# A gated linear attention feeding a mixture of experts: transposed q and k of four chunks in half tiles, the gate's loads behind chunk 0's, and a new order of the first steps

## The chip, the core and the metric

The kernel runs on one core of a Trainium2 chip. The core has a tensor engine for matmuls (PE in the profile, PEld for its weight loads), a vector engine (DVE), a scalar engine (ACT), a GpSimd engine (POOL), and a sync engine whose queue (SP) issues all of this kernel's data transfers. Each engine works through its own list of instructions in order; semaphores make one wait for another. The metric is the device time of one execution in microseconds (us), the median of several runs.

## The reference

```python
def _attn_ref(q, k, v, alpha):            # q, k, v, alpha: [4, 8, 768, 48]
    state = np.zeros((B, H, D, D))
    for t in range(S):
        state = alpha[:, :, t, :, None] * state + np.einsum('bhd,bhe->bhde', k[:, :, t], v[:, :, t])
        y[:, :, t] = np.einsum('bhd,bhde->bhe', q[:, :, t], state)
    return y

def _moe_ref(x, w_gate, w1, w2):          # x: [3072, 384], 8 experts, hidden width 1024
    logits = x @ w_gate
    P = np.exp(logits - logits.max())
    for _ in range(8):
        P /= P.sum(1, keepdims=True) + 1e-09
        P /= P.sum(0, keepdims=True) + 1e-09
        P *= N / E
    for e in range(E):
        out += P[:, e:e + 1] * (np.maximum(x @ w1[e], 0.0) @ w2[e])
    return out
```

The attention's output, 3072 tokens of 8 heads by 48, is the `x` of the mixture of experts. All eight experts see all tokens, so the matmuls of the experts are most of the work.

## The kernel before

**Attention.** The 768 steps of a sequence are cut into chunks of 128 tokens, 24 chunks over the four sequences. Within a chunk the products of decays are built up by doubling: at level L (1, 2, 4, 8, 16, 32, 64) the scores between the two halves of each block of 2L tokens are made by matmuls, and then q's second halves and k's first halves are multiplied by the decays of the other half, in place. The first four chunks do this with q and k already transposed (`direct_chunk`, line 328); the others start from blocks of 16 tokens that DVE and POOL work out in the natural layout (`attn_block`, line 448, two chunks at once), go through DRAM and continue in `attn_chunk` (line 589). Both end in `attn_tail` (line 656), which adds the carried state, scales the result into two float16 tiles `xT` (a high and a low part) and works out the logits of the gate.

**A direct chunk, step by step.** A step is what runs up to the next `yield`. "c0.3" is the third step of chunk 0.

- Step 1 (lines 335 to 338): SP issues five loads, alpha into `AN`, k into `KN`, q into `QN`, and v in two parts.
- Step 2 (341 to 359): PE transposes alpha, k and q, four transposes each, one for each pair of heads (`psD`, `psTk`, `psQR`); ACT copies each result out of PSUM, and DVE multiplies q by alpha. q and k lie side by side in one tile `T2` ("T" in the profile), 4 pairs of heads by 128 tokens each.
- Step 3 (361 to 422): 64 matmuls of 32 by 32 scores into `psl`; DVE multiplies them by a mask into `A32` (shown as "A<-psl,same"). Then level 1.
- Steps 3 to 7, levels 1 to 16 (407 to 422): 64 small matmuls into other columns of `psl`; DVE takes the scores of the level before over into `A32` (`kept`, the profile's COPY_PREDICATED "A<-odd,psl"); `merge` (380) multiplies pairs of decays (`D`, on POOL in steps written with a capital letter, else on DVE) and then, in one DVE instruction of 128x512 elements, the halves of q and k ("T<-T,D").
- Steps 8 and 9, levels 32 and 64 (425 to 445): 16 and 8 matmuls, a merge each, and ACT copies into `A`.
- Steps 10 to 13: `attn_tail`. Step 12 writes `xT`, step 13 the logits, which need the gate's weights.

**Experts.** `load_expert` (line 165) brings in an expert of the first three: steps w0.1 and w0.2 issue the loads of w1 (16 transfers) and w2 (2 transfers) into rooms that later hold `xT`; two steps of squares on ACT, one that finds a scale, then four steps that split a quarter of w1 each into a high part (ACT) and a low part (DVE in steps written small, POOL after two ACT operations in steps with a capital letter). w0.9 ends w1, w0.16 ends w2. `moe_tile` (line 241) computes one expert for 128 or 256 tokens in pieces of PE work ("ps" in the profile); the results go to DRAM as `raw`. These pieces are the filler: a step "f" runs so many of them as 0.45 us of PE work stands for, if any are ready. A tile becomes ready when its expert's w1 is split and the `xT` of its tokens is written; its second half waits for w2.

**The order.** One list, `START` (line 40), says in which order the steps of the chunks (c), blocks (b), experts' weights (w), decays (d), gate (g) and filler (f) are written out, up to chunk 7; from there a repeated unit `UNIT` takes over. A step that comes too soon (`early_`, line 811) is put off. Each engine gets its instructions in this order. After the attention, the sinkhorn loop (line 877) and five more experts follow with matmuls alone (`first`, `second`), from about 815 us on.

**The gate.** `work_gate` (line 218) takes the four loads of the gate's weights, issued by SP at line 764 ahead of everything in `START`, through a maximum and a scale to two float16 tiles, in three steps g.1 to g.3.

Of the kernel before, what the change touches and what calls it, by code (L numbers as in the profile page):

```python
# [25 lines left out]
def tile_gla_moe(ctx: ExitStack, tc: tile.TileContext, q, k, v, alpha, wg, w1, w2, out):  # L26
# [301 lines left out]
    def direct_chunk(ch, got):  # L328
# [10 lines left out]
        yield  # L339

        def turned(x, tag, t=None):
# [38 lines left out]
        def merge(L, Dl, both=True):  # L380

            n = P // (2 * L)
            d = Dl.rearrange("p j (n z) -> p (j n) z", z=2)
# [1 line left out]
            (GE if lop[0] else VE).tensor_mul(Dn.rearrange("p j n -> p (j n)"), d[:, :, 0], d[:, :, 1])

            x = T2.rearrange("p a j (n z t) -> p a (j n) z t", z=2, t=L)
            if both:
                e = x[:, 0, 0, 1, 0]
                o = bass.AP(tensor=e.tensor, offset=e.offset,  # L390
                            ap=[e.ap[0], [NP * P - L, 2], [2 * L, NP * n], [1, L]])
                m = bass.AP(tensor=d.tensor, offset=d.offset, ap=[d.ap[0], [1, 2], [2, NP * n], [0, L]])
                VE.tensor_mul(o, o, m)
            else:
                o = x[:, 1, :, 0]
                VE.tensor_mul(o, o, d[:, :, 1:2].to_broadcast([P, NP * n, L]))
            return Dn
# [9 lines left out]
        for i in range(NLV):  # L407
# [3 lines left out]
            for j in range(NP):  # L411
                for g4 in range(4):
                    tok = slice(g4 * 32, (g4 + 1) * 32)
                    for r in range(2):
# [877 lines left out]
```

## Time and profile before

| | us |
|---|---|
| median of 3 runs | 1712.93 |
| lowest and highest run | 1710.33, 1715.35 |
| the profiled execution: its time | 1712.7 |
| its span, first to last instruction | 1711.0 |
| its ACT busy | 932.9 |
| its POOL busy | 340.4 |

The span is 1.7 us shorter than the time of that execution. In the rows of a timeline stand: start, duration, engine, line, operation, "output<-inputs", partitions by elements, the number of instructions merged into the row, and in brackets how long the engine had been idle and what ended it ("issue": nothing that the profile shows). Most lines are L58 or L67, those of two helpers that record every operation, so the tiles' names are what one goes by. A row that merges many matmuls gives the time from the first to the last.

### The profile page before, as it was taken

How to read it: one execution, taken by the hardware profiler on the slowest of the kernel's cores; microseconds unless marked ns; L12 is line 12 of the kernel's file. 1: busy time of each engine (PE TensorE's matmuls, PEld its weight loads, DVE VectorE, ACT ScalarE, POOL GpSimd, SP SyncE). 2: the span in 40 equal slices, each digit the busy share in tenths (PEclk: the TensorE clock that was granted, in tenths of full speed). 3: DMA queues.
4: the chain of work that ended last, by engine and by line, in shares of the span. 5: the costliest groups of instructions: out<-in, count | busy, mean ns of one | idle time of the engine just before them, and what ended most of it. 6: DMA issues, size and time to landing. Idle time of an engine off the chain costs nothing.

```text
span 1711.0 us, 54791 instructions
## 1 busy us (share of the span) xinstructions
PE 1619.5 (95%) x23585; PEld 1438.3 (84%) x23585; DVE 1277.9 (75%) x2983; ACT 932.9 (55%) x2246; POOL 340.4 (20%) x345
## 2 busy tenths in 40 slices
PE   5679999999999999999899999999999999999998
PEld 4566677777777777767799999999999999999998
DVE  4757777666666656356788989998899979887776
ACT  3457443333333333326677767766666666665554
POOL 3334255434443533038100000000000000000000
PEclk9889999999999999999999999999999999999999
DMA  7152441342244133021312142323332232111111
GB/s 179 39 135 88 100 94 39 90 101 68 57 105 99 46 78 74 20 61 61 87 56 94 49 121 85 122 85 104 99 124 69 66 84 94 57 57 57 57 57 48
DMA packets 175457, 137.19 MB, mean 80 GB/s; under 512 B 109808, under 2 KB 165360, under 8 KB 175216
## 3 DMA queue, kind: packets, MB, share of 16 engines
q1 hardware_dynamic: 175216, 133.71, 28.3%
q8 instruction: 184, 3.01, 0.7%
q14 instruction: 57, 0.47, 0.1%
HBM read 86.50 MB, written 47.17 MB: 78 GB/s over the span
## 4 chain that ended last, share of the span: by engine, by line
PE 71%; DVE 16%; ACT 4%; issue 4%; DMA 3%; POOL 2%; SPq 1%; ACTq 0%; DVEq 0%; POOLq 0%
PE ps L67 23%; PE p1a L67 11%; PE p2x L67 11%; PE p2y L67 6%; PE p1c L67 5%; PE p1d L67 4%; PE p2v L67 3%; DVE h L58 3%; PE psl L67 2%; PE psy L67 2%; DVE AB L58 2%; POOL tmp L58 2%; DMA w1f<-in_moe_w_dram 2%; DVE tmp L58 1%; ACT w L58 1%
## 5 line engine op out<-in xcount | busy, mean ns | idle before, releaser
L67 PEld LDWEIGHTS <-h 128*128 128x128 f16 x6768 | 579.6, 98 | 115.9 <-issue 10.8
L67 PEld LDWEIGHTS <-w 128*128 128x128 f16 x8424 | 598.9, 98 | 43.2 <-issue 9.4
L58 DVE TENSOR_TENSOR h<-hf,h 128x256 f16<-128x256 f32 x480 | 290.5, 616 | 31.2 <-ACT h L58 30.8
L67 PE MATMUL ps<-xT,w 128*128 128x256 f16 (+1 forms) x2664 | 303.9, 271 | 7.2 <-DVE h L58 3.8
L67 PE MATMUL ps<-w,h 128*128 128x384 f16 x1728 | 293.6, 327 | 4.1 <-DVE w L58 2.2
L67 PE MATMUL p2x<-w,h 128*128 128x192 f16 x2880 | 276.8, 246 | 3.6 <-DVE p2y L58 3.4
L58 ACT CAST h<-hf 128x256 f16<-128x256 f32 x480 | 252.1, 571 | 13.1 <-DVE hf L58 8.4
L58 DVE TENSOR_TENSOR hf<-hf 128x256 f32<-128x256 f32 x480 | 182.1, 421 | 50.1 <-ACT hf L58 45.7
L58 DVE SCALAR_TENSOR_TENSOR h<-ps,h 128x256 f16<-128x256 f32 (+1 forms) x296 | 116.1, 411 | 138.2 <-ACT h L58 137.6
L58 ACT ACTIVATE h<-ps 128x256 f16<-128x256 f32 (+1 forms) x296 | 109.1, 375 | 143.5 <-PE ps L67 142.7
L67 PE MATMUL p1a<-xT,w 128*128 128x128 f16 x2160 | 179.5, 219 | 0.0
L67 PEld LDWEIGHTS <-wx 128*128 128x128 f16 x2160 | 147.8, 98 | 17.6 <-issue 17.5
L67 PE MATMUL p1c<-xT,w 128*128 128x128 f16 x2160 | 160.5, 220 | 0.0
L58 POOL TENSOR_TENSOR tmp<-qt,kt 128x768 f32<-128x768 f32 (+1 forms) x80 | 125.2, 1568 | 160.8 <-DVE AB L58 86.8
L58 ACT ACTIVATE hf<-p1d 128x256 f32<-128x256 f32 x120 | 45.8, 382 | 178.9 <-DVE h L58 148.8
L58 ACT COPY r<-ps 128x384 f32<-128x384 f32 x72 | 34.3, 478 | 194.1 <-PE ps L67 151.8
L67 PE MATMUL p2y<-w,h 128*128 128x192 f16 x1440 | 138.5, 246 | 1.2 <-ACT p2y L58 1.2
L67 PE MATMUL p1a<-xc,wx 128*128 128x128 f16 x1440 | 120.3, 220 | 15.3 <-ACT v L58 14.9
L58 DVE TENSOR_REDUCE AB<-tmp 128x16 f32<-128x768 f32 (+2 forms) x90 | 80.7, 904 | 49.0 <-POOL tmp L58 48.7
L67 PE MATMUL p1d<-xT,w 128*128 128x128 f16 x720 | 79.7, 220 | 0.0
L67 PE MATMUL p1d<-xT,wx 128*128 128x128 f16 x720 | 79.5, 220 | 0.0
L67 PE MATMUL p1a<-xc,w 128*128 128x128 f16 x720 | 79.4, 219 | 0.0
(208 smaller groups left out, 1969.4 us busy)
## 6 DMA issues: line engine op xcount, KB each, us to landing
accd<-acc SPq DMA_DIRECT2D x48, 384.0 KB, 2.5
acc<-accd SPq DMA_DIRECT2D x48, 384.0 KB, 3.3
raw<-r SPq DMA_DIRECT2D x72, 192.0 KB, 1.9
ri<-raw SPq DMA_DIRECT2D x72, 192.0 KB, 3.3
w1f<-in_moe_w_dram SPq DMA_DIRECT2D x20, 384.0 KB, 7.0
w2f<-in_moe_w_dram SPq DMA_DIRECT2D x5, 1536.0 KB, 7.2
VN<-in_v_dram SPq DMA_DIRECT2D x48, 96.0 KB, 3.1
xT<-in_moe_w_dram SPq DMA_DIRECT2D x6, 768.0 KB, 5.3
```

What stands on the lines that cost most here:

```text
L58: r = f(*a, **k_)
L67: tc.keep_in_program_order(nc.tensor.matmul(out_, lhsT, rhs, start=start, stop=stop, **k_))
```

## The change

Three edits go together.

First, `T2` becomes a list of two tiles, `T0` and `T1`, each with q and k of two pairs of heads. The copy of k out of PSUM and the product of q with alpha are made in two halves; every level writes the 32 matmuls of one half, that half's multiplication, then the 32 matmuls of the other half, `kept` and the second multiplication; the product of the decays comes last. The arithmetic and the number of matmuls stay.

```diff
-        T2 = fp.tile([P, 2, NP, P], F32, tag="T", name=f"T_{nm}")
-        QT, KT = T2[:, 0], T2[:, 1]
-        turned(kn[:, c], "Tk", KT)
+        HJ = NP // 2
+        T2 = [fp.tile([P, 2, HJ, P], F32, tag=f"T{z}", name=f"T{z}_{nm}") for z in range(2)]
+        psk, _ = turned(kn[:, c], "Tk", T2, 1)
         psq, QR = turned(qn[:, c], "QR")
-        VE.tensor_mul(QT.rearrange("p j t -> p (j t)"), psq, Dl.rearrange("p j t -> p (j t)"))
+        for z in range(2):
+            VE.tensor_mul(T2[z][:, 0], half(psq, z), Dl[:, z * HJ:(z + 1) * HJ])
...
         for i in range(NLV):
             L = 1 << i
...
-            for j in range(NP):
-                for g4 in range(4):
-                    tok = slice(g4 * 32, (g4 + 1) * 32)
-                    for r in range(2):
...
-            if i:
-                kept(i - 1)
-            Dl = merge(L, Dl)
+            Dn, part, deeper = merge(L, Dl)
+            for z in range(2):
+                Qz = odds(z, L)
+                for jj in range(HJ):
+                    for g4 in range(4):
+                        tok = slice(g4 * 32, (g4 + 1) * 32)
+                        for r in range(2):
+                            pr = slice(r * DP, r * DP + D)
+                            o = (z * HJ + jj) * P + 32 + i * 16
+                            mm(psl[r][tok, o:o + 16].rearrange("p (n t) -> p n t", t=L), T2[z][pr, 1, jj, tok],
+                               Qz[pr, jj, g4 * w:(g4 + 1) * w])
+                if z and i:
+                    kept(i - 1)
+                part(z)
+            deeper()
+            Dl = Dn
             yield
```

`part(z)` is the multiplication of `merge` for one of the two tiles, and `deeper` the product of the decays; levels 32 and 64 are rewritten in the same way.

Second, the gate's four loads become the first step of `work_gate`, which now has four steps; step 13 of a direct chunk waits for the fourth.

```diff
     def work_gate(wgf):
+        for j in range(NP):
+            SP.dma_start(wgf[quarter(j)], rows_of(wg, j))
+        yield
...
     hold[0] = True
-    for j in range(NP):
-        SP.dma_start(wgf[quarter(j)], rows_of(wg, j))
...
-            return (n == 12 and m < ND and gates[0] < 3 or m >= ND and "dtot" not in got[m // NCH]
+            return (n == 12 and m < ND and gates[0] < 4 or m >= ND and "dtot" not in got[m // NCH]
```

Third, `START` is another list. Up to the step that writes chunk 3's `xT` the two lists run as follows; a capital letter is one of the list's, f(n) are n pieces of filler, and the f's that find nothing to run are left out. Before:

```
c0.1 C0.2 C0.3 C0.4 C1.1 c0.5 C1.2 C0.6 w0.1 c0.7 B2.1 C1.3 C2.1 W0.2 w0.3 c0.8 c1.4 w0.4 W0.5 C1.5 w0.6
c0.9 w0.7 C1.6 w0.8 C0.10 C2.2 C1.7 b2.2 C0.11 w0.9 W1.1 c1.8 c2.3 B2.3 C1.9 W0.10 C3.1 C1.10 B2.4 g.1
B2.5 b2.6 c2.4 c0.12 c1.11 f(2) b2.7 f(2) b2.8 f(4) c2.5 c1.12 w0.11 b2.9 C3.2 c2.6 C3.3 c2.7 c2.8 w0.12
C3.4 c2.9 W0.13 c3.5 c2.10 b2.10 w0.14 w0.15 c3.6 b2.11 g.2 W0.16 W1.2 W1.3 W1.4 f(8) W1.5 f(4) C3.7 f(4)
B2.12 C3.8 b2.13 B2.14 B2.15 c3.9 g.3 c0.13 c2.11 C2.12 C1.13 W1.6 W1.7 c3.10 c3.11 C3.12
```

After:

```
c0.1 c1.1 C0.2 c0.3 C0.4 c0.5 c1.2 g.1 w0.1 w0.2 c0.6 w0.3 c0.7 W0.4 c0.8 w0.5 c2.1 C1.3 C0.9 c1.4 C1.5
w0.6 b2.1 w0.7 w0.8 w0.9 w1.1 c1.6 c0.10 C2.2 B2.2 C1.7 C1.8 C0.11 B2.3 g.2 C1.9 b2.4 w0.10 c2.3 C1.10
b2.5 c3.1 c2.4 B2.6 c0.12 c1.11 f(2) b2.7 f(6) c2.5 B2.8 C2.6 C1.12 c3.2 W0.11 b2.9 C3.3 c2.7 W0.12 C2.8
c3.4 c3.5 W0.13 c2.9 B2.10 w0.14 w0.15 C2.10 b2.11 g.3 B2.12 c3.6 W0.16 W1.2 w1.3 W1.4 f(11) w1.5 C3.7 f(4)
C3.8 f(1) B2.13 B2.14 b2.15 C3.9 g.4 C0.13 C2.11 c2.12 c1.13 W1.6 C3.10 C3.11 C3.12
```

Behind that the list goes on to chunk 7 with small shifts of the same kind; the pieces of filler up to the step that writes chunk 7's `xT` are as many as before. `attn_tail` takes q and k as lists of pairs of heads, with no change of what it does.

More of the change, by code (lines that the diff above doesn't have):

```diff
@@ L339, in direct_chunk, with turned @@
         yield
-        def turned(x, tag, t=None):
+        half = lambda x, z: x.rearrange("p (z j t) -> p z j t", z=2, t=P)[:, z]
+        def turned(x, tag, t=None, a=0):
             ps = psa.tile([P, 512], F32, tag="psa", name=f"ps{tag}_{nm}")
@@ L384, in merge, with part @@
             Dn = fp.tile([P, NP, n], F32, tag=f"D{2 * L}", name=f"D{2 * L}_{nm}")
[L385 to L397, printed above, removed]
+            def part(z):
+                x = T2[z].rearrange("p a j (n z t) -> p a (j n) z t", z=2, t=L)
+                dz = d[:, z * HJ * n:(z + 1) * HJ * n]
+                if both:
+                    e = x[:, 0, 0, 1, 0]
+                    o = bass.AP(tensor=e.tensor, offset=e.offset,
+                                ap=[e.ap[0], [HJ * P - L, 2], [2 * L, HJ * n], [1, L]])
+                    m = bass.AP(tensor=dz.tensor, offset=dz.offset, ap=[dz.ap[0], [1, 2], [2, HJ * n], [0, L]])
+                    VE.tensor_mul(o, o, m)
+                else:
+                    o = x[:, 1, :, 0]
+                    VE.tensor_mul(o, o, dz[:, :, 1:2].to_broadcast([P, HJ * n, L]))
+            return Dn, part, lambda: (GE if lop[0] else VE).tensor_mul(Dn.rearrange("p j n -> p (j n)"),
+                                                                      d[:, :, 0], d[:, :, 1])
         def kept(i):
@@ L426, in direct_chunk @@
             room = [x.rearrange("p (j c) -> p j c", c=P)[:, :, at_:at_ + L] for x in psl]
-            Qz = QT.rearrange("p j (n z t) -> p j n z t", z=2, t=L)[:, :, :, 1]
-            Kz = KT.rearrange("p j (n z t) -> p j n z t", z=2, t=L)[:, :, :, 0]
-            for j in range(NP):
-                for n in range(P // (2 * L)):
-                    po = slice(n * 2 * L, n * 2 * L + L)
-                    for r in range(2):
-                        pr = slice(r * DP, r * DP + D)
-                        mm(room[r][po, j], Kz[pr, j, n], Qz[pr, j, n])
-            Dl = merge(L, Dl, L < 64 or ch > 0)
+            Dn, part, deeper = merge(L, Dl, L < 64 or ch > 0)
+            for z in range(2):
+                Qz = odds(z, L)
+                Kz = T2[z][:, 1].rearrange("p j (n z t) -> p j n z t", z=2, t=L)[:, :, :, 0]
+                for jj in range(HJ):
+                    for n in range(P // (2 * L)):
+                        po = slice(n * 2 * L, n * 2 * L + L)
+                        for r in range(2):
+                            pr = slice(r * DP, r * DP + D)
+                            mm(room[r][po, z * HJ + jj], Kz[pr, jj, n], Qz[pr, jj, n])
+                part(z)
+            deeper()
+            Dl = Dn
             if L == 32:
@@ L445, in direct_chunk @@
             yield
-        yield from attn_tail(0, ch, vn[:, c], KT, QT, A, Dl[:, :, 0])
+        K_, Q_ = ([T2[j // HJ][:, a, j % HJ] for j in range(NP)] for a in (1, 0))
+        yield from attn_tail(0, ch, vn[:, c], K_, Q_, A, Dl[:, :, 0])
     def attn_block(b, u, got):
@@ L653, in attn_chunk @@
         yield
-        yield from attn_tail(b, ch, vn[:, c], KT, QT, A, got["dtot"][:, c])
+        K_, Q_ = ([x[:, j] for j in range(NP)] for x in (KT, QT))
+        yield from attn_tail(b, ch, vn[:, c], K_, Q_, A, got["dtot"][:, c])
     def attn_tail(b, ch, vn, KT, QT, A, dtot):
@@ L683, in attn_tail @@
             for j in range(NP):
-                tr(psk[:, j * P:(j + 1) * P], KT[:, j], ident)
+                tr(psk[:, j * P:(j + 1) * P], KT[j], ident)
             kb = ap2.tile([P, NP, P], F32, tag="kb", bufs=1, name=f"kb_{nm}")
@@ L763, in tile_gla_moe @@
     hold[0] = True
-    for j in range(NP):
-        SP.dma_start(wgf[quarter(j)], rows_of(wg, j))
     done = [99] * (ND // NCH) + [0] * (len(units) - ND // NCH)
```

19 lines of the change are left out of this document (10 added, 9 removed).

## The prediction

> **What bounds the kernel now.** I began with the page's first part, which says how much of the span each engine works.
>
> ```profile
> span 1711.0 us, 54791 instructions
> PE 1619.5 (95%) x23585; PEld 1438.3 (84%) x23585; DVE 1277.9 (75%) x2983; ACT 932.9 (55%) x2246; POOL 340.4 (20%) x345
> ```
>
> PE is idle for 1711.0 - 1619.5 = 91.5 us, and its work does not change here. Second came the table of busy time by stretch (start and end, length, then PE, PEld, DVE, ACT and POOL with their counts, PE's granted clock, DMA share, GB/s), cut where the stages change.
>
> ```profile
> 0.00:9.40 9.40, 2.88 (x12) 2.24 (x12) 2.49 (x12) 3.23 (x5) 7.65 (x35) 1.00 0.65 122
> 9.40:37.00 27.60, 14.95 (x766) 12.86 (x766) 13.59 (x36) 10.85 (x24) 2.33 (x5) 1.00 0.80 204
> 37.00:62.00 25.00, 17.99 (x463) 13.75 (x454) 13.80 (x31) 10.72 (x25) 7.89 (x9) 1.00 0.41 98
> 62.00:97.00 35.00, 21.78 (x731) 17.75 (x731) 27.62 (x68) 18.18 (x42) 15.29 (x14) 0.80 0.09 25
> 97.00:122.00 25.00, 18.79 (x332) 15.01 (x331) 13.84 (x45) 12.27 (x32) 8.47 (x8) 0.86 0.58 135
> 122.00:171.00 49.00, 45.02 (x506) 34.16 (x505) 33.94 (x73) 32.19 (x76) 19.74 (x16) 0.97 0.39 109
> 815.00:1711.00 896.00, 871.01 (x13007) 864.56 (x13005) 760.75 (x1891) 591.60 (x1361) 2.48 (x3) 1.00 0.26 80
> ```
>
> Half of the idle time, 122 - 76.4 = 45.6 us, lies ahead of 122 us; behind it PE is 92% busy and more. The reason is in the timeline of PE: the experts' first matmul comes at 61.67, but only two small tiles can be filled in until chunk 3's xT is written, and the large tiles begin behind it.
>
> ```profile
> 61.67 0.23 PE L67 MATMUL ps<-xT,w 128*128 128x128 f16 x1
> 122.66 9.58 PE L67 MATMUL ps<-xT,w 128*128 128x256 f16 x71 [0.55 <-DVE xT L58]
> ```
>
> So the first 122 us are bound by the way to chunk 3's xT (steps c0.1 to C3.12), not by PE's work. Every us taken from that way moves the rest forward, and the change touches little else. The waits of PE in that stretch (us in total, times, longest) show of what the way is made:
>
> ```profile
> PE psl L67 <- DVE A L58: 12.0, 7, 5.2
> PE psl L67 <- issue: 6.4, 4, 3.4
> PE psl L67 <- DVE T L58: 4.4, 5, 1.5
> ```
>
> PE's small matmuls wait 16.4 us for DVE (the merges T and the takeovers A), which is what the half tiles aim at, and 6.4 us for nothing that the profile shows.
>
> **Part 1, the gate's loads.** They are the first thing on SP, 1.81 us; behind the change they follow chunk 1's loads. Chunk 0's loads start 1.8 us earlier.
>
> ```profile
> 0.80 1.81 SPq L58 DMA_DIRECT2D wgf<-in_moe_w_gate_dram  x4
> 2.65 0.43 SPq L58 DMA_DIRECT2D AN<-in_alpha_dram  x1
> 4.88 0.56 POOL L58 MEMSET KN<- 128x256 f32 x2
> 5.87 1.09 PE L70 MATMUL psD<-ident,AN 128*128 128x128 f32 x4 [5.87 <-DMA AN<-in_alpha_dram]
> 6.75 1.06 PE L70 MATMUL psTk<-ident,KN 128*128 128x128 f32 x4
> ```
>
> Alpha's transposes wait for their load, but k's, at 6.75, also need POOL's zeroing of KN, which ends at 4.88 + 0.56 = 5.44 and stays. The gain is at most 6.75 - 5.44 = 1.3, and I take **-1.3**; its ends are -1.8 and 0. Nothing is lost behind: expert 0's loads on SP follow c0, c1 and the gate in either order, and the gate's weights are first used far later.
>
> **Part 2, the half tiles.** Two levels of chunk 0 while it runs alone, in the timeline of all engines:
>
> ```profile
> 9.40 0.69 DVE L58 TENSOR_TENSOR T<-psQR,D 128x512 f32<-128x512 f32 x1 [5.46 <-ACT QR L58]
> 10.83 0.84 PE L67 MATMUL psl<-T 48*32 48x16 f32 x64 [0.52 <-DVE A L58]
> 12.45 0.84 PE L67 MATMUL psl<-T 48*32 48x16 f32 x64 [0.79 <-DVE T L58]
> 13.33 0.44 DVE L58 COPY_PREDICATED A<-odd,psl 128x128 f32<-128x128 int32 x1 [0.93 <-PE psl L67]
> 13.57 0.72 DVE L58 TENSOR_TENSOR T<-T,D 128x512 f32<-128x512 f32 x1
> 14.35 0.40 PE L67 MATMUL psl<-T 48*32 48x16 f32 x18 [1.05 <-DVE T L58]
> ```
>
> A level takes 14.35 - 12.45 = 1.90: matmuls 0.84, takeover, merge. With halves the first merge runs beside the second 32 matmuls, and the second merge beside the next level's first 32. But the row at 10.83 shows matmuls held by a DVE read of other columns of the same psl (T was ready at 9.40 + 0.69 = 10.09), so the takeover stays between two levels: 0.84 + 0.44 + about 0.08 of handing over = 1.36. Gain 0.54 a level, where a chunk runs alone. Where DVE is the one that is late, it pays instead:
>
> ```profile
> L58 DVE TENSOR_TENSOR T<-T,D x28: 418/686/991, 11.7 to 110.9; 128x512 f32<-128x512 f32 x27, 128x256 f32<-128x256 f32 x1
> 62.00:97.00 35.00, 9.86 (x588) 8.27 (x588) 7.44 (x11) 0.59 (x1) 0.80 0.09 25
> L58 ACT COPY T<-psTk x4: 585/586/588, 7.8 to 71.7; 128x512 f32<-128x512 f32 x4
> L58 ACT ACTIVATE h<-ps 128x256 f16<-128x256 f32 x5 | 1.9, 383 | 5.2 <-PE ps L67 5.2
> ```
>
> The group of T (ns: least, median, most) has 0.686 for 512 elements and 0.418 for the one of 256: each split adds 2 x 0.418 - 0.686 = 0.150. There are 32 (28 merges, 4 products with alpha), 4.8 us in all. Between 62 and 97 DVE is busy 27.62 of 35 us and sets the pace; the second row, that stretch for tile T alone, counts 11 there: 11 x 0.15 = **+1.6**. In 37 to 62 and 97 to 122 I put some ten splits (+1.5) against three levels alone (-1.6), nothing. ACT's copy of k in halves costs 2 x 0.383 - 0.586 = 0.2, from the nearest ACT row of 256 elements, on the path for chunk 0: **+0.2**.
>
> In 9.4 to 37, where chunk 0 mostly runs alone, seven levels would give 7 x 0.54 = 3.8. Something else is late there:
>
> ```profile
> q8 instruction: 184, 3.01, 0.7%
> 15.38 0.69 PE L67 MATMUL psl<-T 48*32 48x16 f32 x46 [0.63 <-issue]
> 30.43 0.43 PE L67 MATMUL psl<-T 48*32 48x16 f32 x28 [3.37 <-issue]
> 32.15 2.27 PE L67 MATMUL psl<-T 48*32 48x16 f32 x98 [0.77 <-DVE T L58]
> 36.45 0.68 PE L67 MATMUL psl<-T 48*32 48x16 f32 x46 [2.02 <-issue]
> ```
>
> The instructions come by DMA in packets of 3.01 MB / 184 = 16.4 KB. From the stop at 30.43 to the one at 36.45 PE runs 28 + 98 matmuls and the two of a scale between, 128, each with a weight load: 256 instructions, one packet if each has 64 bytes. So PE stops where its next packet has not come, beside data loads that keep the DMA engines 0.80 busy. Here a packet came after 36.45 - 30.43 = 6.0 us; two levels at the new pace need 2 x 1.36 = 2.7. There PE is paced by its code, and shorter levels only wait longer for it. I take **-1.0**, two levels' worth, nearer to this row than to the 3.8; the ends are -3.8 and +9.1 (the second rival).
>
> The Trainium skill speaks otherwise on this: Runtime: NRT & Kernel Launch, section Instruction fetch mechanics, names blocks of 256 instructions, as the count here agrees, and says "The cost of crossing a 16 KiB boundary is one DMA tail-bump, mostly hidden". The 3.37 us disagree. By that rule the stage would come out as in the first rival.
>
> **Part 3, the order.** Expert 0's last quarter of w1 (w0.9) moves from behind C0.11 to ahead of c1.6. In the timeline it stands between chunk 0's state and chunk 1:
>
> ```profile
> 48.50 0.93 ACT L58 ACTIVATE w<-xT,s_w 128x768 f16<-128x768 f32 x1
> 49.47 1.02 DVE L58 SCALAR_TENSOR_TENSOR w<-xT,s_w,w 128x768 f16<-128x768 f32 x1 [0.61 <-ACT w L58]
> 50.68 0.72 PE L67 MATMUL psl<-T 48*32 48x32 f32 x28 [2.93 <-DVE A L58]
> ```
>
> PE waits 2.93 behind it; 0.93 + 1.02 = **-2.0** goes. In its new place PE waits for packets, which covers it; without that cover it costs the 2.0 again. What is late next is chunk 2's turning and the block's work on DVE. w0.2's two loads pass ahead of c2.1 and b2.1 on SP: they lengthen the time in which packets are slow, but chunk 2 is turned only behind c0.10 in both orders. The step c3.2 passes ahead of W0.11 and b2.9, which held PE here:
>
> ```profile
> 79.29 1.62 PE L67 MATMUL psl<-T 48*32 48x16 f32 x128 [5.18 <-DVE A L58]
> ```
>
> Up to 5.2 could go; but the same DVE work then stands ahead of c2.7 and W0.12, and DVE has hardly a gap. I take 0, with ends -5.2 and +1.6 (the splits once more). The D products that go over to POOL and the later W1.7 fall beside PE's or DVE's work.
>
> **The sum**: -1.3 - 1.0 + 1.6 + 0.2 - 2.0 = -2.5. From the profiled execution's 1712.7 (span 1711.0 and 1.7 around it): **1710.2**. The median of the runs shown, 1712.93, is 0.2 above that execution. A measurement of this kernel tells about 0.3%, 5.1 us, from no change, so this would be no difference.
>
> **The rivals.**
>
> 1. *The packets keep up, and the halves pay everywhere.* If half of the 16.4 - 2.93 = 13.5 us of waits for DVE goes (-6.7), the sum is -1.3 - 6.7 + 1.6 - 2.0 = -8.4: **1704.3**. For it: the three waits behind 10.83 are of that kind, and in 62 to 97 the DMA share is 0.09 and no stop is seen. Against: the 6.0 us a packet.
> 2. *The packets fall behind* (the other side). PE reaches each end of a packet earlier, while the loads of w0.2 are in flight right behind those of w0.1. If the three ends that now cost little (0.63, 0.38 by difference of the 6.4, and one without a stop between) cost 3.37 each, that is 10.1 - 1.0 = +9.1, and with the rest -1.3 + 1.6 + 0.2 - 2.0 the time is **1720.3**. It is slower by over 0.3% once these three wait some 7.7 us in all. Against: a packet asked for earlier may also come earlier.
> 3. *DVE is the bound throughout*: all 32 splits on the path, nothing from the levels: -1.3 + 4.8 + 0.2 - 2.0: **1714.4**. The busy row of 62 to 97 speaks for it, those around it against. The Trainium skill, VectorE: DVE Perf Modes, section The TRN2 errata, has the same mechanism, "a single large tile pays it once; many small tiles pay it per-tile"; the 0.150 here agrees.
> 4. *The halves do not do what they are for*: the takeover holds both, and the levels stay at 1.90: 1710.2 + 1.0 = **1711.2**.
>
> **How the numbers follow.** Forecast 0.42, of which 0.08 lies below 1707.8; first rival 0.30, second 0.16, third 0.07, fourth 0.05. Faster by over 0.3%: 0.30 + 0.08 = 0.38; within: 0.34 + 0.07 + 0.05 = 0.46; slower 0.16. Both signs hold much, so the forecast's own range is 1706.5 to 1714. The range for 8 in 10 takes in the first rival with 2 us to spare and stops a little short of the second: 1702 to 1719.
>
> **What would show it.** Right, step by step: k's first transposes near 5.4; chunk 0's levels 1.36 apart where no stop stands between; stops by "issue" every 128 small matmuls up to 37, as long as now or longer; no w between chunk 0's state and chunk 1's level; more DVE time in T by 4.8; the 128x256 matmuls of tokens 256 to 511 near 120. Wrong: stops gone, or that start ahead of 116 or behind 124, or PE's idle time behind 122 changed by over 3 us.

## The result, and the profile after

The changed kernel takes 1700.31 us (median of 4 runs, 1699.28 to 1702.97), the kernel before, in the same comparison, 1714.14 (4 runs, 1710.33 to 1715.56). The ratio is 0.9925, with a 95% interval of 0.9904 to 0.9946. That is faster by more than the 0.3% that a measurement of this kernel can tell, and the 1700.31 lies 9.9 us below the forecast and 1.7 below its range. A repeat beside other runs (e5 below) gave 0.9939 [0.9925, 0.9952].

The first part of the page of the changed kernel:

```profile
span 1698.3 us, 54817 instructions
PE 1619.8 (95%) x23585; PEld 1441.0 (85%) x23585; DVE 1266.9 (75%) x3011; ACT 935.5 (55%) x2251; POOL 346.9 (20%) x349
```

PE's work is the same, and it is idle for 78.5 us in place of 91.5. Where the idle time went is seen in the table of busy time by stretch, cut at the same times as before:

```profile
0.00:9.40 9.40, 3.88 (x86) 2.99 (x93) 3.67 (x15) 3.29 (x6) 5.99 (x32) 1.00 0.85 165
9.40:37.00 27.60, 13.71 (x691) 11.72 (x691) 15.18 (x48) 11.61 (x26) 2.40 (x5) 0.69 0.74 191
37.00:62.00 25.00, 17.65 (x491) 13.92 (x475) 15.61 (x41) 9.84 (x25) 9.94 (x12) 0.64 0.40 96
62.00:97.00 35.00, 25.80 (x763) 21.59 (x762) 30.15 (x77) 19.87 (x47) 14.87 (x14) 0.77 0.17 53
97.00:122.00 25.00, 20.58 (x335) 16.53 (x335) 13.31 (x47) 13.92 (x31) 6.71 (x9) 0.86 0.59 131
```

Ahead of 122 us PE is busy for 3.88 + 13.71 + 17.65 + 25.80 + 20.58 = 81.6 us, so idle for 40.4, against 45.6 before: 5.2 less. Behind 122 it is idle for 78.5 - 40.4 = 38.1, against 91.5 - 45.6 = 45.9: **7.8 less in the part that the prediction left alone**. A change of over 3 us there was one of the signs of being wrong that it named.

Fixed times mix stages that have moved. So from here on the stretches are cut where the program itself has marks: at the first "psy<-A,VN", the matmuls of the scores with v of a chunk. In that measure, before (the same view; the columns after the length are PE, PEld, DVE, ACT and POOL busy):

```profile
37.06:57.02 19.96, 13.05 (x339) 10.09 (x336) 10.40 (x24) 9.23 (x22) 3.48 (x5) 1.00 0.42 105
87.96:116.61 28.65, 21.94 (x406) 16.42 (x400) 17.30 (x52) 16.68 (x40) 10.17 (x9) 0.92 0.46 120
152.55:195.51 42.96, 38.22 (x463) 28.39 (x454) 31.91 (x61) 25.41 (x56) 13.97 (x11) 1.00 0.39 102
362.23:717.63 355.40, 350.81 (x4594) 268.99 (x4589) 217.38 (x430) 133.50 (x371) 135.96 (x110) 1.00 0.31 74
255.46:820.70 565.24, 552.38 (x6799) 420.75 (x6792) 355.59 (x724) 219.99 (x589) 239.98 (x232) 1.00 0.28 69
```

and after:

```profile
37.29:54.76 17.47, 12.19 (x339) 9.58 (x335) 9.63 (x28) 8.36 (x22) 5.39 (x7) 0.60 0.55 132
85.86:111.66 25.80, 22.33 (x408) 16.87 (x404) 18.57 (x55) 16.00 (x38) 8.39 (x10) 0.90 0.41 122
146.70:185.09 38.39, 37.34 (x462) 28.52 (x458) 29.61 (x60) 24.46 (x55) 13.71 (x8) 1.00 0.25 78
357.88:710.97 353.09, 352.11 (x4607) 270.30 (x4602) 214.40 (x433) 135.75 (x373) 136.67 (x110) 1.00 0.30 74
244.64:806.20 561.56, 553.55 (x6800) 421.55 (x6793) 345.71 (x719) 220.10 (x588) 241.31 (x231) 1.00 0.28 71
```

The rows are: chunk 0 to 1; 2 to 3; 4 to 5; 11 to 23; and, with that one in it, all from chunk 7 to the first matmul of the five experts behind. Chunk 0 comes no earlier (37.29, in the timeline below, against 37.06). Then three stretches are shorter: by 2.5 (0 to 1), 2.85 (2 to 3) and 4.6 (4 to 5). In the first of them PE's idle time fell by only 1.6 (19.96 - 13.05 = 6.91 to 17.47 - 12.19 = 5.28); the rest is matmuls that took less time, of which the last section tells more. The long one, chunk 11 to 23, lost most of PE's idle time (355.40 - 350.81 = 4.59 before, 353.09 - 352.11 = 0.98 after), and all from chunk 7 on is 565.24 - 561.56 = 3.7 shorter, though more of the filler, the matmuls of the first experts, now falls ahead of chunk 11 (by 33 recorded matmuls). These four make 13.6 of the 14.5 us by which the first matmul of the five experts comes earlier (806.20 against 820.70). The stage of these experts itself took 1.8 longer (1698.3 - 806.2 = 892.1 against 1711.0 - 820.7 = 890.3), which leaves 12.7.

How chunk 0 runs, in the timeline of PE of the changed kernel:

```profile
5.24 1.11 PE L70 MATMUL psTk<-ident,KN 128*128 128x128 f32 x4
...
9.32 0.84 PE L67 MATMUL psl<-T 48*32 48x16 f32 x64 [0.52 <-DVE A L58]
10.37 0.84 PE L67 MATMUL psl<-T 48*32 48x16 f32 x64 [0.21 <-DVE T L58]
12.16 0.39 PE L67 MATMUL psl<-T 48*32 48x16 f32 x18 [0.95 <-DVE A L58]
...
25.03 0.59 PE L67 MATMUL pst_w<-w1m,ones 128*128 128x4 f32 x2 [3.68 <-ACT w L58]
...
37.29 1.93 PE L67 MATMUL psy<-A,VN 128*32 128x128 f32 x32
...
59.07 0.23 PE L67 MATMUL ps<-xT,w 128*128 128x128 f16 x1
...
117.66 1.58 PE L67 MATMUL ps<-xT,w 128*128 128x256 f16 x13 [0.55 <-DVE xT L58]
```

k's transposes start at 5.24, 1.5 earlier. Between there and the scores the gain is lost: at 25.03 PE stands 3.68 us before the two matmuls of a scale, which it did not before. They are step w0.5 of expert 0, which the new order has ahead of chunk 1's level 1, and they wait for ACT's squares of weights whose load is still under way.

### The profile page after: what moved, and what is told of

Its sections match the earlier page's. It is cut to its first block, busy times and chain, and to the rows that moved or that the text cites. A ratio compares the mean times of both kernels' runs of the same rounds, so it can differ in the third digit from the quotient of the medians.

```text
span 1698.3 us, 54817 instructions
## 1 busy us (share of the span) xinstructions
PE 1619.8 (95%) x23585; PEld 1441.0 (85%) x23585; DVE 1266.9 (75%) x3011; ACT 935.5 (55%) x2251; POOL 346.9 (20%) x349
## 4 chain that ended last, share of the span: by engine, by line
PE 76%; DVE 11%; ACT 4%; issue 3%; DMA 3%; POOL 2%; SPq 2%; ACTq 0%; DVEq 0%; POOLq 0%
PE ps L67 27%; PE p1a L67 12%; PE p2x L67 11%; PE p2y L67 6%; PE p1c L67 6%; PE p1d L67 4%; PE p2v L67 3%; PE psy L67 2%; PE psl L67 2%; DVE h L58 2%; SPq L58 2%; DMA w1f<-in_moe_w_dram 2%; POOL tmp L58 2%; ACT w L58 1%; DVE hf L58 1%
## 5 line engine op out<-in xcount | busy, mean ns | idle before, releaser
L58 POOL TENSOR_TENSOR tmp<-qt,kt 128x768 f32<-128x768 f32 (+2 forms) x82 | 132.0, 1616 | 140.8 <-DVE AB L58 73.0
L58 ACT ACTIVATE hf<-p1d 128x256 f32<-128x256 f32 x120 | 45.8, 382 | 178.2 <-DVE h L58 149.5
```

Of the source, the lines that this page charges most:

```text
L58: r = f(*a, **k_)
```

## The experiments

Steps are named as in the prediction. Medians have those of the kernel before, run beside them, in brackets. Where lists were edited, the executed order was written out in full, so that nothing else moves. One thing about the profiles: in executions with the same first steps (before, e6, e8, e9, e13) chunk 0's scores come between 35.12 and 37.06, so that a difference under 2 us at that mark tells nothing. Most stretches from there on repeat to some 0.3. But chunk 0 to 1 differs by 1.1 between the changed kernel (17.47) and e3 (18.55), which has the same first steps, and chunk 2 to 3 by 1.0 among the executions with the old order.

**e1, the halves alone**: the two tiles in the old order, the gate's loads first.

```diff
-        T2 = fp.tile([P, 2, NP, P], F32, tag="T", name=f"T_{nm}")
+        T2 = [fp.tile([P, 2, HJ, P], F32, tag=f"T{z}", name=f"T{z}_{nm}") for z in range(2)]
```

> The half tiles with the order of before, and the gate's loads in front as before. Theory (the first stage is paced by the instruction packets and by DVE, so the halves pay little by themselves): -2 us against before, between -4 and +2, and chunk 0's score matmuls with v (psy) at 37 as before. Rival (the halves are the gain, wherever PE waits for DVE): -6 to -8 us, psy of chunk 0 at 33.

Measured: 1711.98 us (1711.04), ratio 1.0006 [0.9998, 1.0015]. Chunk 0's scores come at 36.74, chunk 1's 18.92 later (19.96 before), chunk 2's 31.19 (30.94). Alone the halves change nothing that can be measured: PE's idle time from chunk 0 to 1 is 6.94, as long as before.

**e2, the order alone**: the new list and the gate's loads in their new place, with the whole tile.

```diff
-    START = 'c0 C0 C0 C0 f C1 ...'
+    START = 'c0 c1 C0 c0 f f C0 ...'
```

> The new order and the gate's loads in their new place, with q and k in one tile as before. Theory (the order is the gain, before chunk 3 and behind it): -8 to -11 us, chunk 3's psy near 113 against 116.6. Rival (the order was found for short levels and needs them): between -3 and +5 us, chunk 3's psy at 117 or later.

Measured: 1702.73 (1711.04), ratio 0.9950 [0.9936, 0.9963]. The stretches from chunk 2 to 3 (25.86) and 4 to 5 (38.40) are those of the changed kernel, so both come of the order. Only from chunk 1 to 2 it is worse: 33.30, against 31.10 with the halves. The theory held: by the ratio the order alone brings 8.6 us.

**e3 and e4, the order in two parts**, both with the halves. e3 has the new order up to C3.12 and the old one behind; e4 the old one (and the gate first) up to C3.12 and the new one behind.

```diff
 e3: START = <new, c0.1 to C3.12> + w1.7 + <old, behind C3.12>
 e4: START = <old, c0.1 to C3.12> + <new, behind C3.12, without w1.7>
```

> The changed kernel with the new order up to the step that writes chunk 3's xT, and from there the old order (with the one step w1.7 that it still lacks put first). Theory (half of the gain is in the order behind chunk 3): -5 to -7 us, and chunk 5's psy 75 to 79 us behind chunk 3's, as before. Rival (all of it starts ahead of chunk 3, and what came behind only follows): -11 to -13 us.

> The reverse: half tiles, gate's loads in front, the old order up to chunk 3's xT and the new one behind it. Theory: what the halves give and 5 to 6 us more, -6 to -8 us, chunk 5's psy about 73 us behind chunk 3's. Rival (the order behind chunk 3 gives nothing by itself): what the halves give alone, within 1 us of the run with the halves only.

Measured: e3 1706.77 (1711.04), ratio 0.9977 [0.9967, 0.9986]; e4 1705.48, ratio 0.9968 [0.9956, 0.9981]. e3 has the shorter stretch from chunk 2 to 3 (25.92), e4 that from chunk 4 to 5 (38.39). By their ratios the two parts are worth 3.9 and 5.5 us, 9.4 together; the change as a whole is worth 10.4 by the ratio of e5. Each falls a little short of its theory. The part behind chunk 3's xT is worth at least as much as the part ahead of it, as the idle times (7.8 against 5.2) say too; the intervals of e3 and e4 overlap, so that the runs alone don't tell which is larger.

**e5, the changed kernel again**, beside the runs that follow.

> The changed kernel itself, on one chip with the next three, for a narrower interval. The runs with one part each gave -0.1 (halves), -8.5 (order), -3.9 and -5.5 (order up to chunk 3 and behind it) out of 1711. Theory (the parts add, and the halves pay about 2 us under the new order): -10 to -12 us. Rival (the parts only add up): -9.4 us or less.

Measured: 1699.10 (1711.03), ratio 0.9939 [0.9925, 0.9952]; chunk 0's scores at 37.08.

**e6, ten pieces of filler more.** The stretch from chunk 11 to 23 is the repeated unit, which the change leaves alone. What it meets there is the filler at another point of its own cycle. So the kernel before, with ten steps f at the end of the list:

```diff
-    START = '...'
+    START = '... f f f f f f f f f f'
```

> The kernel before with nothing changed but ten more f behind the last step of START, so that the repeated unit meets the filler 4.8 us of planned work further on, as it does in the changed kernel. Theory (PE's waits for DVE Tq between chunk 11's and chunk 23's psy, 4.6 us of idle time, hang on where the pieces of filler fall in the unit): that idle time falls to 1 or 2 us, and the total by 2 to 5 us. Rival (they went for another reason): idle time there stays at 4.6 and the total within 1 us.

Measured: 1706.87 (1711.03), ratio 0.9982 [0.9973, 0.9990]. The stretch of e6 from chunk 11 to 23, by busy time:

```profile
364.23:717.41 353.18, 352.09 (x4606) 270.27 (x4602) 215.47 (x433) 136.42 (x374) 136.52 (x110) 1.00 0.31 75
```

PE's idle time there falls from 4.59 to 353.18 - 352.09 = 1.09, nearly as in the changed kernel. So this part of the gain is where the filler stands against the unit: an edit that does nothing but shift it brings as much.

**e7, the scale later.** The changed kernel with w0.4 behind C1.3 and w0.5 behind c1.4:

```diff
-... w0.3 c0.7 W0.4 c0.8 w0.5 c2.1 C1.3 C0.9 c1.4 C1.5 ...
+... w0.3 c0.7 c0.8 c2.1 C1.3 W0.4 C0.9 c1.4 w0.5 C1.5 ...
```

> The changed kernel with w0.4 (two squares) behind C1.3 and w0.5 (the scale, a matmul on PE) behind c1.4, as in the old order; else the new order. In the changed kernel PE stood 3.7 us before that matmul, at 25, for squares that waited for the load. Theory (the wait is covered by the instruction packets that are late anyway): chunk 0's psy stays within 1.5 us of 37.3, the total within 2 us of the changed kernel. Rival (the early scale costs what PE waits there): chunk 0's psy near 34, the total 2 to 4 us below the changed kernel.

Measured: 1694.48 (1711.03), ratio 0.9909 [0.9896, 0.9923], 4.6 us below e5, and faster than both kernels. Chunk 0's scores come at 33.71, and the stretches behind are those of e5 within 0.2. The rival held: the early scale cost what PE waits for it. In its place stands another wait (timeline of e7):

```profile
22.23 2.39 PE L67 MATMUL psl<-T 48*32 48x16 f32 x100 [0.37 <-DVE A L58]
28.72 0.66 PE L67 MATMUL psl<-T 48*32 48x16 f32 x44 [4.10 <-issue]
```

PE stops for 4.10 us with nothing to wait for but its instructions. What the DMA engines did from 24 to 29, in the view of the queues of e7 (their busy tenths in 40 slices, and the queue of the instructions: packets, megabytes, share):

```profile
DMA  9999999999999999999999999999999999831110
...
q8 instruction: 1, 0.02, 1.3%
```

All engines are full, and of what they move one packet is instructions; the stop ends at 28.72, in the slices where the data run out. That one packet came late behind the data is what the row suggests; when PE's sequencer asked for it is not in the trace.

**e10 and e12, the loads about that stop.** Both start from e7. In e10 the loads of chunk 2 and block 2 come behind w1.1; in e12 they come ahead of the 1.5 MB of expert 0's second weights.

```diff
 e7:  ... w0.1 w0.2 c0.6 ... c0.8 c2.1 C1.3 ... w0.6 b2.1 w0.7 ... w0.9 w1.1 c1.6
 e10: ... w0.1 w0.2 c0.6 ... c0.8 C1.3 ... w0.6 w0.7 ... w0.9 w1.1 c2.1 b2.1 c1.6
 e12: ... w0.1 c2.1 b2.1 w0.2 c0.6 ... c0.8 C1.3 ... w0.6 w0.7 ... w0.9 w1.1 c1.6
```

> The version with the scale later (e7), with chunk 2's five loads and block 2's three issued behind w1.1 in place of ahead of chunk 0's level 32. Theory (PE's stop of 4.10 us at 28.7 is instructions that come late beside these loads, whose issues SP shows held for 1.8 to 3.1 us each): that stop falls under 1.5 us and chunk 0's scores by v come at 30 to 32 in place of 33.71. Chunk 2 is then turned later, so the whole may gain little: total between -3 and +3 us against e7. Rival (the stop comes of expert 0's loads alone): the stop stays above 3 us, the scores at 33 to 34.

> The version with the scale later (e7), with the loads of chunk 2 and block 2 issued ahead of the loads of expert 0's second weights, which in the old order too came behind chunk 2's loads. Theory (any megabytes in flight delay the instructions): the 4.10 us stop stays within 1 us, now beside the 1.5 MB of the second weights; chunk 0's scores by v at 33 to 35, and the total within 2 us of e7. Rival (it is the many small packets of the chunk's loads that hold the instructions up, not the bytes): the first stop, at 13, grows to over 2 us, as the small packets come earlier, and the one at 28.7 falls under 2 us.

Measured: e10 1707.54 (1712.42), ratio 0.9971 [0.9959, 0.9982]; e12 1697.29 (1712.42), ratio 0.9904 [0.9887, 0.9921]. e10's stop is 2.68 long and chunk 0's scores come at 31.69, 2.0 earlier than e7's, as the theory had it; the stretch to chunk 1 then takes 29.22 in place of 17.35, as this row of its timeline tells:

```profile
43.52 1.09 PE L70 MATMUL psD<-ident,AN 128*128 128x128 f32 x4 [8.85 <-DMA AN<-in_alpha_dram]
```

Chunk 2's loads are late and hold PE for 8.85, and the whole is some 11 us slower than e7, not within 3. Neither theory of e10 was right on the stop: it fell, but not under 1.5; only the loads of the weights are under way in it. e12's stop, in the timeline of PE, and then the DMA engines from 24 to 26:

```profile
25.14 0.66 PE L67 MATMUL psl<-T 48*32 48x16 f32 x44 [0.76 <-issue]
...
30.41 1.93 PE L67 MATMUL psy<-A,VN 128*32 128x128 f32 x32
```

The DMA engines:

```profile
DMA  3322111000000032337798799999999999665533
```

The same two groups of matmuls stand on either side of the stop as in e7; here the engines are nearly empty when PE comes to it, and it takes 0.76 in place of 4.10. My theory for e12 (any megabytes in flight) had expected the long stop, and fell; the rival had the first stop grow past 2 us, and that stayed at 0.46. It would follow that the stop is set by how full the engines are when PE comes to it, but e11 below does not agree with that.

The shorter stop didn't show in the total: chunk 0's scores come 3.3 earlier than in e7, but the intervals of e7 and e12 lie almost on each other.

**e11, the gate's loads alone.** The kernel before, with the gate's loads behind chunk 1's.

```diff
-g.1 c0.1 C0.2 C0.3 C0.4 C1.1 c0.5 ...
+c0.1 C0.2 C0.3 C0.4 C1.1 g.1 c0.5 ...
```

> The kernel before, with the gate's loads alone moved behind chunk 1's loads. The prediction's first part: k's transposes at about 5.4 in place of 6.75, and 1.3 us less, ratio 0.9992. Rival (the gain at the start is lost at the first stop for instructions, which come by DMA beside the same loads): the transposes are 1.3 us earlier, but chunk 0's scores by v stay within 0.4 us of 37.06 and the time within 0.5 us of before.

Measured: 1707.74 (1712.42), ratio 0.9975 [0.9965, 0.9985]: neither 1.3 nor nothing, but 4.7 us at the medians. Timeline of PE of e11:

```profile
24.57 0.43 PE L67 MATMUL psl<-T 48*32 48x16 f32 x28 [0.64 <-issue]
...
31.14 0.69 PE L67 MATMUL psl<-T 48*32 48x16 f32 x46 [1.03 <-issue]
31.75 1.94 PE L67 MATMUL psy<-A,VN 128*32 128x128 f32 x32
```

It runs the same matmuls to the same ends of packets as the kernel before. But it comes to the one of 3.37 us at 24.57 - 0.64 = 23.9 in place of 30.43 - 3.37 = 27.1. Of chunk 2's loads the one of q is the longest in SP's queue, before and in e11:

```profile
23.81 4.03 SPq L58 DMA_DIRECT2D QN<-in_q_dram  x1
```

```profile
25.01 4.05 SPq L58 DMA_DIRECT2D QN<-in_q_dram  x1
```

Before, PE comes to the end of its packet late in that row (27.1, and the row runs to 27.84), in e11 ahead of it (23.9), and the stop is 0.64. It isn't for free engines: the DMA engines' busy share in e11 is 0.90 in the microsecond ahead of that stop and 1.00 in it. Nine executions have this same end of a packet, with 28 matmuls behind it. Where PE comes to it within SP's row of q, the stop is 3.02 to 3.92 (before, e1, e6, e8, e13); behind that row, 1.96 and 1.45 (e4, e9); ahead of it, 0.64 and 0.56 (e11, e16). So the stop goes with the load that SP is issuing; by what way one delays the other is not shown.

All stops of e11 together are 0.64 + 1.03 = 1.7 in place of 6.4. In return PE waits 2.25 for the scale, at 27.25, where it did not wait before. Chunk 0's scores come 3.4 to 5.3 earlier than in the executions with the old start (31.64 in e16, which has this start too).

**e14, the changed kernel with the gate's loads first again.**

```diff
-c0.1 c1.1 C0.2 c0.3 C0.4 c0.5 c1.2 g.1 w0.1 ...
+g.1 c0.1 c1.1 C0.2 c0.3 C0.4 c0.5 c1.2 w0.1 ...
```

> The changed kernel, with the gate's loads first again. Theory (in the changed kernel the early w0.5 holds PE for the load of expert 0's w1, which is issued in the same place either way, so that the gate's move gains nothing there): chunk 0's scores by v stay within 1 us of 37.29, and the time within 1.5 us of the changed kernel's, ratio to before 0.992 to 0.995. Rival (the gate's move is worth the same 4.7 us in either order): the scores at 40 to 42 and the time at 1703 to 1706, ratio 0.995 to 0.997.

Measured: 1699.99 (1711.80), ratio 0.9929 [0.9916, 0.9943], within the interval of e5. Chunk 0's scores come at 37.03. The theory holds: in the changed kernel the gate's move brings nothing at chunk 0, as the scale holds PE until expert 0's load has come, which is as late either way: its matmuls start at 25.96, and at 25.03 in the changed kernel.

**e15, the whole tile in e12's order.**

```diff
-        T2 = [fp.tile([P, 2, HJ, P], F32, tag=f"T{z}", name=f"T{z}_{nm}") for z in range(2)]
+        T2 = fp.tile([P, 2, NP, P], F32, tag="T", name=f"T_{nm}")
```

> The order with the scale later and expert 0's second weights later (e12), but with the whole tile of q and k in place of the halves. Theory (the halves pay where a chunk runs alone and nothing else holds PE, which is so in this order: levels 1.36 apart in place of 1.90): chunk 0's scores by v 1 to 3 us later than 30.41, those of chunk 2 2 us more behind those of chunk 1 (33 in place of 31.60), and the time 2 to 5 us above e12's, ratio to before 0.992 to 0.9935. Rival (as in the old order, where they changed nothing): within 1 us of e12, ratio 0.990 to 0.991.

Measured: 1698.92 (1711.80), ratio 0.9931 [0.9918, 0.9943], against 0.9904 [0.9887, 0.9921] with the halves. The intervals only just meet, and the medians are 1.6 apart. The stretches from chunk 1 to 2, of e15 and then of e12:

```profile
51.38:85.42 34.04, 20.87 (x732) 18.36 (x727) 27.92 (x62) 13.94 (x33) 15.92 (x14) 0.70 0.01 3
```

```profile
48.95:80.55 31.60, 20.96 (x730) 18.31 (x725) 27.18 (x73) 12.71 (x33) 12.23 (x13) 0.72 0.08 17
```

Here the halves are worth 2.4 us, with 11 more instructions on DVE and yet less of its time, as they were worth 2.2 in the changed kernel's own order (33.30 in e2, 31.10 with them). Chunk 0's scores come at 30.41 in place of 32.70, which is little more than that mark varies by itself. In the old order the same stretch was as long with them as without (31.19 in e1, 30.94 before).

**e8 and e9, expert 1's weights ahead of chunk 4's merges**, one piece of what is different between chunks 4 and 5, in the kernel before.

```diff
-... w1.13 W1.14 c4.3 c4.4 w1.15 c4.5 w1.16 C3.13 w2.1 ... w2.10 b3.8 b3.9 ...
+... w1.13 w1.14 w1.15 c4.3 c4.4 w1.16 C3.13 w2.1 ... w2.10 b3.8 c4.5 b3.9 ...
```

In e8 w1.16 moved past 94 steps f as well; in e9 they stay ahead of it.

> The kernel before with five steps moved as the new order has them: expert 1's w1.14 (its low part now on DVE) and w1.15 ahead of c4.3, w1.16 ahead of c4.5, and c4.5 behind b3.8. Theory (between chunk 4's and chunk 5's psy PE waited for the splits and squares of experts 1 and 2, written too late): that stretch falls from 43.0 to 39 or 40 us, and the total by 2 to 4 us. Rival (the 4.6 us come from the whole of the new order there): the stretch stays above 42.

> The kernel before, with one thing of the new order: expert 1's last three steps of weights (w1.14 to w1.16) ahead of c4.3 and c4.4, c4.5 behind b3.8, and every f in its old place against w1.16. Theory (the 4.57 us between the scores by v of chunk 4 and chunk 5 are gained because PE no longer waits there for the splits of weights and for chunk 4's DVE work at once): that stretch falls from 42.96 to 38.4 to 40, and the time by 2 to 4.6 us, ratio 0.997 to 0.999. Rival (it is another part of the order there, the squares of expert 2 or the block's steps): the stretch stays above 42 and the time is the same within 1.5 us.

Measured: e8 1736.62 (1711.03), ratio 1.0151 [1.0137, 1.0165]; e9 1711.08 (1712.42), ratio 0.9996 [0.9985, 1.0007]. e8 shows another thing than it was meant to. Its stretch from chunk 4 to 5 took 65.48, with only 9 more matmuls recorded than before (472 against 463), but with PE idle for 65.48 - 43.34 = 22.1 us, half of it one wait of 11.3 for DVE's tile `deck` of chunk 5. Chunk 5's first matmuls come 45.8 us into the stretch in place of 35.0, behind more of the filler, and no matmul of the filler stands between them and the next scores. e9 has it right, and the rival held for the stretch (e9, from chunk 4 to 5 and 5 to 7):

```profile
152.17:194.24 42.07, 38.38 (x463) 28.43 (x455) 33.49 (x62) 24.35 (x55) 13.87 (x10) 1.00 0.40 104
194.24:255.68 61.44, 58.52 (x723) 43.53 (x727) 44.18 (x83) 26.93 (x75) 29.11 (x22) 0.97 0.42 98
```

0.9 is gained in the first. The second is 61.44 - 59.95 = 1.5 longer than before (255.46 - 195.51 = 59.95), but not by any wait: PE is idle for 2.92 in it before (59.95 - 57.03) and in e9 (61.44 - 58.52). The same 723 matmuls took longer, at a granted clock of 0.97 in place of 1.00, in an execution of 1714.68 where the median of e9 is 1711.08. So nothing shows that the 0.9 was given back, as the expectation of e13 takes it; the ratio is too coarse to tell 0.9 from nothing.

**e13, the new order between w2.9 and b3.16 alone**, in the kernel before.

```diff
-w2.9 w2.10 b3.8 b3.9 B3.10 B3.11 B3.12 c4.6 b3.13 w2.11 b3.14 B3.15 c5.1 c5.2 w2.12 w2.13 c5.3 w2.14 c5.4 w2.15 c5.5 w2.16
+w2.9 b3.8 B3.9 B3.10 c5.1 B3.11 b3.12 w2.10 b3.13 c4.6 B3.14 w2.11 c5.2 b3.15 w2.12 w2.13 W2.14 c5.3 C5.4 w2.15 c5.5 w2.16
```

> The kernel before, with the new order only between the step w2.9 and the step b3.16, that is between the scores by v of chunks 4 and 5 (c4.5 and w1.17 keep their old places). Theory (the gain of that stretch lies in these steps: c5.1 to c5.5 are written ahead of the last steps of block 3 and of expert 2's splits): the stretch falls from 42.96 to 38.4 to 40 and stays gained: 2 to 4 us less, ratio 0.9977 to 0.9988. Rival (the stretch becomes shorter, but PE then waits in the next ones, as with expert 1's weights, where 0.9 was gained there and 1.5 lost behind): the time stays within 1.5 us of before.

Measured: 1709.71 (1711.80), ratio 0.9988 [0.9979, 0.9997], 2.1 us less. The stretch:

```profile
151.80:192.53 40.73, 37.66 (x463) 28.51 (x458) 29.06 (x60) 26.05 (x57) 17.43 (x12) 1.00 0.24 75
```

It is 2.2 shorter, a little less than the theory wanted, and the gain stays. What PE waited for there, in the kernel before (us in total, times, longest):

```profile
PE pst_w L67 <- ACT w L58: 1.3, 1, 1.3
PE ps L67 <- DVE w L58: 0.9, 1, 0.9
PE psy L67 <- ACT ab L58: 0.7, 1, 0.7
```

and three smaller ones, one of 0.7 and two of 0.5, the last ended by nothing that the profile shows. In the changed one the longest is:

```profile
PE pss L67 <- ACT kb L58: 0.5, 1, 0.5
```

Six small waits, of which none is longer than 1.3, have gone or shrunk. e9 took the first from 1.3 to 0.2 and the second away, but its wait for DVE's h grew from 0.5 to 1.3; it took the whole new order to be rid of all.

**e16, the two single edits together**: the kernel before with the gate's loads moved (e11) and the ten f's (e6).

```diff
-g.1 c0.1 C0.2 C0.3 C0.4 C1.1 c0.5 ...
+c0.1 C0.2 C0.3 C0.4 C1.1 g.1 c0.5 ... f f f f f f f f f f
```

> The kernel before with the two single edits that gained: the gate's loads behind chunk 1's, and ten pieces of filler more at the end of the list, so that the filler stands otherwise against the repeated unit. Theory (the two lie at places that do not touch each other, the start and the stretch of chunks 11 to 23): the gains add, 4.7 + 3.1 to 4.2 = 8 to 9 us, ratio 0.9948 to 0.9955, which is most of what the whole change brings. Rival (both do the same, move the filler against the unit, as the f's count PE's time in the order): not over 5 us, ratio 0.997 or above, and PE's idle time between the scores of chunks 11 and 23 as small with one as with both.

Measured: 1703.87 (1711.80), ratio 0.9955 [0.9942, 0.9967], the theory's figure. The gains add: by the ratios 4.3 and 3.1 alone, 7.7 together. The theory holds. And e11 alone leaves PE's idle time between chunks 11 and 23 at 4.53, so it does not move the filler. Two small edits bring 7.7 us, where the whole change brings 10.4 (e5) to 12.9 (the first comparison).

## Why the prediction was wrong, step by step

- **"The change touches little else"** is the step that failed. It set the price of everything behind chunk 3's xT to nothing, and PE lost 7.8 us of idle time there, against 5.2 ahead of it. e4, with the new order there only (and the halves, which bring nothing alone), shows 0.9968 by itself: about 2.1 of it by the steps between chunks 4 and 5 (e13) and 3.1 by the filler's place against the repeated unit (e6). The list is another up to chunk 7, and the steps behind chunk 3 got no price. The page of before already showed what there was to win: PE is idle for 45.9 us from 122 on, of which 896.00 - 871.01 = 25.0 lie in the last stage and were not won, and the 4.74 between chunks 4 and 5 were six waits, five of them for work that an order sets.
- **Part 1, the gate's loads, -1.3**: the mechanism was right and the size was off. k's transposes came at 5.24, as forecast (5.4). But that time was taken as a shift of everything behind. It is a shift against the loads: alone it gave -4.7 (e11), with PE at the end of a packet ahead of chunk 2's load of q in place of within it.
- **Part 3, the rest of the order, 0**: it held the scale. The list has w0.5 ahead of C1.3, where it was behind c1.4, and I priced only w0.9 and w0.2. It costs 3.7 us of PE's time (the row at 25.03), 3.6 of chunk 0's scores (37.29 to 33.71 in e7), and eats all that the gate's move gives (e14). So a gain larger than the -1.3 and a cost that I had at 0 cancelled: chunk 0's scores come at 37.29 against 37.06, where the prediction's terms up to there (-1.3, -1.0 and +0.2) put them 2.1 earlier. The experts' first matmul is 61.67 - 59.07 = 2.6 earlier, which looks like the sum of -2.5. But by the prediction's own terms it had to be 4.1 earlier, as the +1.6 lies behind it, and the large tiles come 122.66 - 117.66 = 5.0 earlier, not 2.5. That agreement was luck.
- **Part 3, w0.9, -2.0**: the stretch from chunk 0 to 1 is 2.5 shorter, but the order gives 1.3 of it (18.69 in e2 against 19.96) and the halves 0.1 (18.55 in e3). In the other 1.1 the changed kernel differs from e3, whose first steps are the same, by transposes of 0.66 in place of 1.12 (last section). The 18.92 of e1 is of that kind too, as its idle time is that of before. The mechanism was right, and the term was too large by a third.
- **Part 3, c3.2, 0 with an end at -5.2**: the wait of 5.18 at 79.29 lies between chunks 1 and 2. In the changed kernel it is one of 4.43 at 76.91, so the 0 was nearly right there. **The steps about chunk 3** had no term: the stretch from chunk 2 to 3 gave -2.85, with the order alone as well (e2), and not with the halves alone (28.57 in e1). The waits of PE in that stretch, before:

```profile
PE psl L67 <- ACT A L58: 2.4, 1, 2.4
PE ps L67 <- POOL w L58: 1.3, 1, 1.3
...
PE ps L67 <- DVE w L58: 0.8, 1, 0.8
```

and after:

```profile
PE psg L67 <- ACT wg L58: 1.5, 1, 1.5
```

  The wait for the scores A and those for splits of weights are gone, and the gate's is the longest left. Which of the steps did it was not tried.
- **Part 2, the levels 1.36 apart**: they are 1.05 and 1.79 (9.32, 10.37, 12.16), against 1.62 and 1.90 before. The takeover does stand between two levels, as forecast. I had not asked in what order DVE comes to its work. DVE of the changed kernel:

```profile
10.57 0.42 DVE L58 TENSOR_TENSOR D<-D 128x256 f32<-128x256 f32 x1
11.09 0.66 DVE L58 TENSOR_TENSOR T<-T,D 128x256 f32<-128x256 f32 x1
11.68 0.43 DVE L58 COPY_PREDICATED A<-odd,psl 128x128 f32<-128x128 int32 x1
```

  The product of decays, written last in the level before, now stands ahead of the first half's multiplication, which ends at 11.75; the takeover ends at 12.11, and the matmuls start at 12.16. It stands on DVE because the new order has c0.3, where the old one has C0.3 with that product on POOL. With the halves in the old order (e1) the same level takes 13.34 - 11.88 = 1.46. So the half tiles do overlap as forecast and gain 0.44 there, not far from 0.54; a level that has its D on DVE gains 0.1. The prediction priced the products that go over to POOL and not those that come back to DVE.
- **Part 2, paced by packets, -1.0 from 9.4 to 37**: the packets do set the pace, and the halves alone brought nothing there that can be told (36.74 in e1). But the size of a stop is no property of the stage: at one end of a packet the runs show 3.37 (before) and 0.64 (e11), at another 4.10 (e7), 2.68 (e10) and 0.76 (e12). At the first of these ends the prediction's "shorter levels only wait longer for it" holds where PE still comes to it while SP is issuing chunk 2's load of q, and not where it comes ahead of that. The Trainium skill, Runtime: NRT & Kernel Launch, section Instruction fetch mechanics, calls the crossing of a block mostly hidden; the 0.64 and 0.76 come near to that, the 4.10 does not.
- **Part 2, the splits, +1.6 and 4.8 in all**: the time in T up to 122 us (the table by stretch, for that tile alone) rose from 22.15 to 28.96, by 6.8. It cost nothing that was seen: the stretch where DVE was to set the pace, chunk 1 to 2, took 31.10 against 30.94, and with the whole tile in the same order 33.30 (e2).
- **The rivals.** The first (1704.3) is nearest in time, for another reason: the waits for DVE did not halve. These are PE's up to 122 us in the changed kernel:

```profile
PE psl L67 <- DVE A L58: 15.1, 13, 4.4
PE psl L67 <- issue: 5.2, 3, 2.5
```

  What PE waited for T before, 4.4, is nearly gone (0.2), and the wait for the takeovers A has grown by 3.1: 15.1 + 0.2 against the 16.4 of both. The second rival needed the packets to fall behind; the stops are 5.2 against 6.4. The third fell with e1. The fourth, that the halves do nothing, is right for the old order by the time (e1), but not by its reason: the levels of e1 are 1.05 and 1.46, not 1.90. For the new order it is wrong (e2, e15).

What stays open: which steps make the 2.85 between chunks 2 and 3, the part of the 4.6 between chunks 4 and 5 that neither e9 (0.9) nor e13 (2.2) gives, and by what way a load's issue makes a stop long.

## What to carry to other kernels

Price every step that a new order moves, the early ones that wait for a load above all: the scale that came too soon hid a gain of some 4 us, and moving it back gave the best kernels here (0.9909 and, with the second weights' load later, 0.9904, which is no difference between the two). Where PE runs small matmuls beside loads, ask at which time it comes to the end of each packet of instructions and which load is being issued then, since a shift of 1.5 us was worth 4.7 here. And before a gain in a part that a change does not touch is explained, shift that part alone by a few pieces of filler, as e6 does: it may be no more than where two cycles stand against each other. And before a longer stretch is put down to a wait, compare PE's idle time in it: in e9 the 1.5 us were slower matmuls, not a wait.

## What the runs showed of the hardware that was not expected

One end of a packet of instructions cost 0.76 (e12), 2.68 (e10) or 4.10 us (e7) with the same matmuls on both sides of it; another cost 0.56 to 3.92 us over nine executions, sorted by where PE came to it against SP's row of one load. How full the DMA engines are does not tell it alone: a stop of 0.64 (e11) had them 1.00 busy, one of 2.68 (e10) 0.83.

The same matmuls run at two paces in the first 60 us, and the granted clock shows it only in part. The four transposes of chunk 2's alpha, in the kernel before:

```profile
40.72 1.12 PE L70 MATMUL psD<-ident,AN 128*128 128x128 f32 x4 [0.68 <-ACT kb L58]
```

and after:

```profile
40.95 0.66 PE L70 MATMUL psD<-ident,AN 128*128 128x128 f32 x4 [0.68 <-ACT kb L58]
```

The column behind POOL's, cut at just these rows, says 1.00 in both (the 0.60 from chunk 0 to 1 after is a mean of the whole stretch). In eight other executions (e2, e3, e6, e8, e9, e11, e12, e15) it says 0.50 at this place, and there the transposes take 1.12 throughout. In after, e1, e4 and e7 it has risen to 1.00 shortly before, and they take 0.66. But in before, e13, e14 and e16, where it has stood at 1.00 from the start, they take 1.12 as well, and in e5 0.66. So the durations follow the column where it has moved, and a 1.00 that has stood from the start tells nothing; there a stage's pace is taken from the durations of its matmuls. The pace is worth 1.1 us from chunk 0 to 1, it differs between executions with the same first steps (0.66 after, 1.12 in e3), and what sets it was not found.
